# Another order for the beginning of a linear-attention and gated-MLP kernel on one Trainium2 core

## The chip, the cores and the metric

The kernel runs on one core of a Trainium2 chip. The metric is the device time of one execution in microseconds. The core has a matrix engine (TensorE, PE in the profile, with its weight loads as PEld), three elementwise engines (VectorE or DVE, ScalarE or ACT, GpSimd or POOL) and SyncE (SP), which issues nearly all transfers here. Each engine works through its own list of instructions in order and waits on semaphores that others raise.

## The reference

Eight batches of 576 tokens, 8 heads of 64. First a linear attention with a norm per head, then a gated MLP with a spatial gate:

```python
kv = np.einsum('bhsd,bhse->bhde', k, v)
out = np.einsum('bhsd,bhde->bhse', q, kv)
rms = np.sqrt(np.mean(out * out, axis=-1, keepdims=True) + 1e-06)
x = out / rms * g_norm                        # per token: 8 heads side by side, 512 wide
h = gelu_tanh(x @ w_in)                       # 512 -> 1024
u, v = h[..., :512], h[..., 512:]
v_n = layer_norm(v) * g_ln
v_s = np.einsum('ts,bsd->btd', w_sg, v_n) + b_sg[None, :, None]
return x + (u * v_s) @ w_out                  # 512 -> 512
```

The result is float32. `w_in` and `w_out` are float64 inputs: the kernel loads them as pairs of 32-bit words and makes float32 values from them on the chip.

## The kernel before, in words

All large products run as three products of rounded parts: each operand is split into a high part (a cast to the matrix engine's fast float32 form) and a low remainder (a subtraction), and high x high, high x low and low x high are summed in PSUM. Tensors lie with channels on the 128 partitions, so x of a batch is four tiles of 128 channels by 576 tokens, and a token half is 288 columns.

The work of one batch, by the letters of the table `ORDER`: k loads k and v, K multiplies them to kv (four blocks of 128 tokens and a last one of 64), c copies kv out of PSUM; q loads q, o multiplies q by kv, e squares the result, f scales it by g_norm into x, s sums the squares per head with a matrix of ones, t makes 1/rms of the sums, M or r spread it over the channels, x multiplies it in, X and Y make x's high and low parts; U and V are the two halves of x @ w_in, S is the spatial product, G the gate, P the last product, Q and Z add it to x, O stores. D, A, B, E, L, C, F, I load and convert the weights: D is the load, A, B, E, L, C make float32 values from the words (on ACT, DVE and POOL), F the high part, I the low one. N is a warm matmul: it multiplies zeros into a PSUM bank that nobody reads.

`ORDER` (line 115 on) is a table written by hand: the program is recorded in that order, so it sets the order in every engine's list, SP's included. `HOMES` says which buffer each new tile takes; a tile waits until the last user of its buffer is done. A letter at a step's end (v, a, p) names its engine.

In batch 0 the tokens are treated in two halves. o(0, n) makes half n // 4 of channel tile n % 4; `sums` collects the four tiles of a half in one PSUM block (lines 463 to 476), `rstd` (line 494 on) makes 1/rms with one ACT step and three DVE steps, `broadcast` (line 548 on) spreads it over 128 channels with the 0/1 matrix `ext` as the stationary operand. All other batches send 1/rms through DRAM and load it back spread.

The beginning in the table before: k and v of batch 0 are loaded block by block with one block of u's words between them, then all of q; all four tiles of half 0 and those of half 1 follow each other closely; u's first step comes after both halves are scaled and after kv of batch 1 and its first o. The k and v of the last 64 tokens are two loads of 64 partitions each, and `ext` is a load of 64 partitions on SP.

Of the kernel before, what the change touches and what calls it, by code (L numbers as in the profile page):

```python
# [58 lines left out]
""",  # L59
    h="""  # L60
# [775 lines left out]
```

## Time and profile before

| | us |
|---|---|
| median of 3 runs | 494.47 |
| lowest, highest run | 493.2, 494.67 |
| span of the profiled execution, first to last instruction | 490.1 |
| PE busy in it | 482.1 (98%) |
| DVE, ACT, POOL busy | 351.3, 179.8, 159.1 |

The time of the profiled execution outside its span is not in the profile; the median run is 4.37 us above the span. The page also cuts the span into 40 slices: PE shows 6 tenths in the first slice and 9 (90% or more) in all others but the last. The chain of work that ended last is PE for 96% of the span and a transfer of k and v for 2%. A line like "L666" is a line of the kernel; a bracket behind an instruction gives the idle time of its engine before it and what ended that. A PE record of a plain float32 matmul counts twice, as it takes two passes. Times in brackets of another engine's rows are idle time there, which costs nothing unless PE waits for what follows.

### The profile page before, as it was taken

To read this page: it belongs to the slowest core of one execution; us is meant where nothing else is said; L and a number is where in the kernel's file an instruction comes from. 1 tells how busy PE (TensorE), PEld (TensorE's weight loads), DVE (VectorE), ACT (ScalarE), POOL (GpSimd) and SP (SyncE) were. 2 spreads that over 40 slices of the span, in tenths; PEclk is the share of its full clock that TensorE was granted. 3 is DMA by queue.
4 is the path that set the end of the run, shared out by engine and by line. 5 is a ranking of instruction groups with operands and counts; after the bars stand their busy time and mean duration, and the time that the engine had idled before them with its cause. 6 is when DMAs were issued, how large, how long until landed. Compare 5 with 4: busy or idle time off the path is not lost.

```text
span 490.1 us, 10060 instructions
## 1 busy us (share of the span) xinstructions
PE 482.1 (98%) x3989; PEld 440.8 (90%) x3989; DVE 351.3 (72%) x809; ACT 179.8 (37%) x442; POOL 159.1 (32%) x204
## 2 busy tenths in 40 slices
PE   6999999999999999999999999999999999999997
PEld 6668889998998999988998998998998899998997
DVE  1698698888777786468765875577767687577576
ACT  1668575155234331142223323335033332123220
POOL 0333142652232323332143113342305232442551
PEclk9999999999999999999999999999999999999999
DMA  8996793054343612064535443300331021100033
GB/s 228 361 353 232 220 277 104 2 157 141 104 142 89 142 43 74 1 192 130 175 75 185 117 104 117 100 1 1 97 104 49 1 62 43 49 1 0 2 122 120
DMA packets 33658, 55.36 MB, mean 113 GB/s; under 512 B 7308, under 2 KB 9228, under 8 KB 33612
## 3 DMA queue, kind: packets, MB, share of 16 engines
q1 hardware_dynamic: 33612, 54.73, 37.1%
q8 instruction: 31, 0.51, 0.4%
q14 instruction: 15, 0.12, 0.1%
HBM read 44.76 MB, written 9.95 MB: 112 GB/s over the span
## 4 chain that ended last, share of the span: by engine, by line
PE 96%; DMA 2%; DVE 0%; ACT 0%; SPq 0%; issue 0%
PE pu L666 21%; PE pg L680 21%; PE pv L615 20%; PE py L741 18%; PE pkv L414 5%; PE pg L683 3%; PE po L439 3%; PE pss L484 2%; DMA kv_first<-in_vx 1%; DMA kv_first<-in_kx 1%; PE psq L468 1%; PE pq L439 1%; PE pb L552 1%; PE warm L270 0%; SPq L405 0%
## 5 line engine op out<-in xcount | busy, mean ns | idle before, releaser
L693 POOL TENSOR_TENSOR u<-gt,u 128x288 f32<-128x288 f32 x64 | 56.3, 890 | 116.3 <-DVE gt L688 113.6
L680 PE MATMUL pg<-wsh,vh 128*128 128x288 f32 x256 | 75.8, 296 | 0.0
L680 PE MATMUL pg<-wso,vh 128*128 128x288 f32 x256 | 75.4, 294 | 0.0
L680 PE MATMUL pg<-wsh,vo 128*128 128x288 f32 x256 | 75.4, 294 | 0.0
L754 DVE SCALAR_TENSOR_TENSOR x<-py,x 128x288 f32<-128x288 f32 x112 | 49.4, 451 | 28.7 <-PE py L741 28.3
L709 DVE TENSOR_TENSOR g<-u,g 128x288 fp32r<-128x288 f32 x112 | 56.2, 517 | 15.7 <-ACT g L230 13.0
L688 DVE SCALAR_TENSOR_TENSOR gt<-pg,glt,b_bc 128x288 f32<-128x288 f32 x64 | 32.3, 512 | 35.2 <-PE pg L683 34.9
L741 PE MATMUL py<-g,woh 128*128 128x288 f32 x256 | 55.9, 295 | 0.0
L230 ACT CAST g<-u 128x288 fp32r<-128x288 f32 x75 | 30.8, 434 | 68.2 <-POOL u L693 52.3
L671 ACT ACTIVATE u<-pu 128x288 f32<-128x288 f32 x64 | 25.7, 411 | 68.3 <-PE pu L666 67.1
L680 PEld LDWEIGHTS pg<-wsh,vh 128*128 128x128 f32 x256 | 48.2, 188 | 0.8 <-DVE gt L688 0.4
L680 PEld LDWEIGHTS pg<-wso,vh 128*128 128x128 f32 x256 | 48.1, 188 | 0.1
L680 PEld LDWEIGHTS pg<-wsh,vo 128*128 128x128 f32 x256 | 48.1, 188 | 0.0
L666 PE MATMUL pu<-xh,wuh 128*128 128x288 f32 x256 | 45.5, 299 | 0.0
L721 POOL TENSOR_TENSOR u<-u 128x288 f32<-128x288 f32 x33 | 29.4, 894 | 49.6 <-DVE g L709 40.9
L666 PE MATMUL pu<-xo,wuh 128*128 128x288 f32 x256 | 44.3, 295 | 0.0
L666 PE MATMUL pu<-xh,wuo 128*128 128x288 f32 x256 | 44.3, 295 | 0.0
L620 ACT ACTIVATE hv<-pv 128x512 f32<-128x512 f32 x32 | 19.0, 598 | 66.5 <-PE pv L615 59.5
L741 PEld LDWEIGHTS py<-g,woh 128*128 128x128 f32 x256 | 42.7, 188 | 0.6 <-issue 0.4
L741 PE MATMUL py<-g,wxh 128*128 128x288 f32 x192 | 41.5, 295 | 0.0
L666 PEld LDWEIGHTS pu<-xh,wuh 128*128 128x128 f32 x256 | 37.6, 188 | 3.7 <-issue 1.9
L741 PE MATMUL py<-g,woo 128*128 128x288 f32 x128 | 37.8, 295 | 0.0
(123 smaller groups left out, 1005.6 us busy)
## 6 DMA issues: line engine op xcount, KB each, us to landing
q<-in_qT SPq DMA_DIRECT2D x32, 288.0 KB, 5.5
out_y<-x SPq DMA_DIRECT2D x28, 288.0 KB, 2.9
bc<-rd SPq DMA_DIRECT2D x28, 256.0 KB, 3.9
k<-in_kx SPq DMA_DIRECT2D x24, 256.0 KB, 4.9
v<-in_vx SPq DMA_DIRECT2D x24, 256.0 KB, 4.8
kv_first<-in_kx SPq DMA_DIRECT2D x8, 256.0 KB, 6.3
kv_first<-in_vx SPq DMA_DIRECT2D x8, 256.0 KB, 5.4
words<-in_wu SPq DMA_DIRECT2D x4, 512.0 KB, 8.4
```

What stands on the lines that cost most here:

```text
L230: e.copy(dst, src) if e is ac else e.tensor_copy(dst, src)
L414: nc.tensor.matmul(part["kv", b][64 * r : 64 * r + 64, n * 64 : n * 64 + 64], k_[b, c][:, h], v_[b, c][:, h], start=(c == 0 and n == 0), s ...
L615: nc.tensor.matmul(pv, a[cc], w[:, cc, :], start=(n == 0), stop=(n == 11))
L666: nc.tensor.matmul(pu[:, :HS], w[:, cc, f], a[b, cc][:, t], start=(i == 0), stop=(i == 11))
L671: ac.activation(u_[b, n], part["u", b, n][:, :HS], AF.Gelu_apprx_tanh, scale=W_UP)
L680: nc.tensor.matmul(ps[:, :HS], a[:, d], w[:, c, t], start=(i == 0), stop=False)
L688: ve.scalar_tensor_tensor(g_[b, n], ps[:, :HS], glt[:, dc : dc + 1], b_bc[:, half(n // 4)], op0=ALU.mult, op1=ALU.add)
L693: po.tensor_tensor(u_[b, n], g_[b, n], u_[b, n], op=ALU.mult)
L709: ve.tensor_tensor(lo, src, f32(hi), op=ALU.subtract)
L721: e.tensor_tensor(dst, x, y, op=ALU.subtract)
L741: nc.tensor.matmul(y_[b, bank][c][:, :HS], wo_block(h, blk, e)[:, block(c)], a, start=(start and i == 0), stop=(i == 5), skip_group_check= ...
L754: ve.scalar_tensor_tensor(xs, y_[b, bank][c][:, :HS], W_UP, xs, op0=ALU.mult, op1=ALU.add)
```

## The change

The table `ORDER` is written anew for the beginning (to the middle of batch 1's steps), with engines chosen step by step from there on, and `HOMES` with it. The code around it changes in these places:

- u's words of the first 256 columns (D00, D01) are loaded ahead of k and v, the second 256 columns later. Half 0 of batch 0's tokens goes ahead through o, squares, sums, 1/rms, broadcast, scaling and splitting; the first u step (U00, which needs half 0 and the first 128 columns only) stands before half 1 is scaled.
- q of half 1 gets buffers of its own (from the `x` group).
- The sums of a half lie in two column blocks of 144 tokens each, so four blocks for both halves; 1/rms then works on 64 partitions of 144 columns, where it was 32 of 288, and the broadcast takes two matmuls of 144 columns for one of 288. `ext` is 128 partitions, zeroed by POOL, its ones loaded by four small loads that ACT issues.
- The last 64 tokens of k and v come in one load `kvl` of 128 partitions (heads in two groups of partitions, k and v side by side), and the last kv block uses two diagonal tiles of the matrix.
- More steps can choose their engine (A, y, w, G, J, W), and nine of the layer-norm steps y go to ACT.

```diff
-WARM = "po1"
+WARM = "po0"
 ORDER = """
-    k01 k02 k04 D21 F21 D23 D02 A02 E02 B02v L02 C02 F02v I02v k00 N899 ... K00 k03 D00 K01 K02 K03 K04 c00a ...
+    D01 B01v N899 N898 N897 N896 N895 N894 A01v E01 D00 A00a B00a E00 N893 ... k00 K00 ... k02 k01 K01 k03 k04 ...
...
+    ext = T([P, 2, NP * P], F32, "wsh", nm="ext")
     def constants():
+        po.memset(ext, 0.0)
+        for j in range(4):
+            ac.dma_start(ext[32 * j : 32 * j + H, j % 2, :], ex)
...
-        elif n == 22:
-            part["ext"] = T([64, NP * P], F32, "hv_left", nm="ext")
-            sy.dma_start(part["ext"], ex)
...
     def load_kv(b, c):
-        if c < NC and b < 2:
+        if c == NC:
+            k_[b, c] = T([P, 2, C // 2], F32, "k", 3)
+            sy.dma_start(k_[b, c], kvl[b])
+            return
+        if b < 2:
             k_[b, c], v_[b, c] = (t[:, c, :] for t in first[b])
...
+                    else:
+                        k, v = (k_[b, c][64 * r : 64 * r + 64, i, n * 64 : n * 64 + 64] for i in range(2))
...
-                        tile_position=(0, 64 * r),
+                        tile_position=(64 * r if c == NC else 0, 64 * r),
...
-        q_[b, p] = T([P, S], F32, *(("q", 4) if b else ("xh", NP)), nm="q")
+        q_[b, p] = T([P, S], F32, *(("q", 4) if b else ("xh", NP) if p < 2 else ("x", 12)), nm="q")
...
-            nc.tensor.matmul(
-                sums_[0, r][32 * r : 32 * r + 32, :HS],
...
-                tile_position=(0, 32 * r),
-            )
+            for j in range(2):
+                at = 64 * r + 32 * j
+                nc.tensor.matmul(
+                    sums_[0, r][at : at + 32, :QS],
+                    ones[:, ZO - 2 * p : ZO - 2 * p + 32],
+                    part["sq", 0, 2 * p + r][:, j * QS : j * QS + QS],
...
+                    tile_position=(0, at),
+                )
...
     def broadcast(b, n):
-        r = slice(32 * (n % 2), 32 * (n % 2) + 32)
...
+        r = slice(64 * (n % 2), 64 * (n % 2) + 64)
+        for j in range(2):
+            nc.tensor.matmul(
+                pb[:, j * QS : j * QS + QS],
+                ext[r, j, block(n // 2)],
+                part["rstd0"][0][r],
...
-    def v_norm(b, c):
+    def v_norm(b, c, e):
         mv, rs = st_[b, c]
-        ve.tensor_scalar(hv_[b, c], hv_[b, c], mv[:, 0:1], rs[:, 0:1], op0=ALU.subtract, op1=ALU.mult)
+        if e is ac:
+            e.activation(hv_[b, c], hv_[b, c], AF.Identity, scale=rs[:, 0:1], bias=mv[:, 2:3])
+        else:
+            e.tensor_scalar(hv_[b, c], hv_[b, c], mv[:, 0:1], rs[:, 0:1], op0=ALU.subtract, op1=ALU.mult)
```

What this does to the engines' lists shows at three places. The first is SP's list from its fifth transfer on, before. The names are those of the loads' tiles (`k_92` and `v_93` are the 64-partition ends of k and v, `words` are weights as 32-bit words, `gnt` and `glt` small vectors).

```order
L405 DMA k_92<-in_kl 64x512
L405 DMA v_93<-in_vl 64x512
L295 DMA gnt_65<-in_gn 128x1
L300 DMA glt_67<-in_gl 128x4
L287 DMA words_100<-in_wu 128x2x512
L405 DMA kv_first_77<-in_kx 128x512
L405 DMA kv_first_78<-in_vx 128x512
```

And SP's list from its first transfer on, in the change; between the second and the third fence row below stand the other six loads of k and v.

```order
L294 DMA words_94<-in_wu 128x2x512
L294 DMA words_107<-in_wu 128x2x512
L415 DMA kv_first_77<-in_kx 128x512
L415 DMA kv_first_78<-in_vx 128x512
...
L408 DMA k_205<-in_kvl 128x512
L445 DMA q_233<-in_qT 128x576
L302 DMA gnt_65<-in_gn 128x1
L445 DMA q_244<-in_qT 128x576
L294 DMA words_258<-in_wu 128x2x512
L445 DMA q_288<-in_qT 128x576
```

Two blocks of u's words moved ahead of all of k and v, the vector `gnt` of g_norm moved behind the first q, and the two 64-partition loads became one.

The second place is PE's list from the first kv block of batch 0 to the second o of batch 1, before:

```order
L270 MATMUL warm<-zeros 128x256 x46
L414 MATMUL pkv<-kv_first 64x64 x32
L414 MATMUL pkv<-v,k 64x64 x8
L270 MATMUL warm<-zeros 128x256 x11
L439 MATMUL pq<-q,kvf 64x288 x10
...
L552 MATMUL pb<-rstd,ext 128x288 x6
L414 MATMUL pkv<-kv_first 64x64 x32
L414 MATMUL pkv<-v,k 64x64 x8
L439 MATMUL po<-q,kvf 64x288 x8
L666 MATMUL pu<-xh,wuh 128x288 x4
```

And PE's list for the same stretch in the change, from its first warm matmuls to the first o of batch 1, behind which the second u step follows (the first one's 12 matmuls are three rows, of which the first stands here):

```order
L277 MATMUL warm<-zeros 128x256 x58
L428 MATMUL pkv<-kv_first 64x64 x8
L277 MATMUL warm<-zeros 128x256 x7
L428 MATMUL pkv<-kv_first 64x64 x24
L428 MATMUL pkv<-k 64x64 x8
...
L484 MATMUL psq<-sq,ones 32x144 x8
...
L569 MATMUL pb<-rstd,ext 128x144 x8
...
L689 MATMUL pu<-xh,wuh 128x288 x4
...
L569 MATMUL pb<-rstd,ext 128x144 x6
...
L453 MATMUL po<-q,kvf 64x288 x8
```

The first u step moved ahead of the last four broadcasts, of the last two kv blocks of batch 1 and of its first o; warm matmuls moved to the front (58 and 7, then 3 and 1, where it was 46, 11, 3 and 9).

The third place is DVE's list in the change, from the scaling of half 0's last two tiles to the last of its four remainders; `rstd_280` and `rstd_279` are here those of half 1, and the first of them waits for ACT's list, where its step stands behind two word steps of another block.

```order
L582 TENSOR_TENSOR x_286<-x_286,pb_330 128x288
L582 TENSOR_TENSOR x_268<-x_268,pb_339 128x288
L520 TENSOR_TENSOR rstd_280<-rstd_279 64x144
L333 TENSOR_SCALAR w64_348<-w64_348 128x512
L601 TENSOR_TENSOR xo_393<-x_266,xh_326 128x288
L522 SCALAR_TENSOR_TENSOR rstd_280<-psq_343,rstd_280 64x144
L601 TENSOR_TENSOR xo_398<-x_312,xh_328 128x288
L601 TENSOR_TENSOR xo_400<-x_286,xh_396 128x288
L524 SCALAR_TENSOR_TENSOR rstd_279<-rstd_280,rstd_279 64x144
L601 TENSOR_TENSOR xo_403<-x_268,xh_381 128x288
```

Before, the same place of DVE's list, from the first scaled tile on, has half 1's 1/rms steps between the first tile's scaling and its cast, and seven scalings (the first three stand here) ahead of the next remainders:

```order
L565 TENSOR_TENSOR x_283<-x_283,pb_323 128x288
L506 SCALAR_TENSOR_TENSOR rstd_287<-psq_306,rstd_287 32x288
L508 SCALAR_TENSOR_TENSOR rstd_286<-rstd_287,rstd_286 32x288
L230 CAST xh_343<-x_283 128x288
L326 TENSOR_SCALAR w64_346<-w64_346 128x512
L330 SCALAR_TENSOR_TENSOR w64_346<-words_330,w64_346 128x512
L584 TENSOR_TENSOR xo_352<-x_283,xh_343 128x288
L565 TENSOR_TENSOR x_265<-x_265,pb_356 128x288
L565 TENSOR_TENSOR x_279<-x_279,pb_341 128x288
L565 TENSOR_TENSOR x_279<-x_279,pb_362 128x288
```

So half 0 now goes through as a group of four, with half 1's steps woven between its remainders.

## Rows read from the trace of the kernel before

**Rows 1.** The page: the span, and busy time of each engine.

```profile
span 490.1 us, 10060 instructions
...
PE 482.1 (98%) x3989; PEld 440.8 (90%) x3989; DVE 351.3 (72%) x809; ACT 179.8 (37%) x442; POOL 159.1 (32%) x204
```

**Rows 2.** Busy time by stretch: us, each engine's busy (x instructions), granted clock, DMA share, GB/s.

```profile
12.39:34.55 22.16, 21.50 (x263) 13.90 (x263) 17.53 (x40) 13.69 (x33) 6.86 (x6) 1.00 1.04 355
34.55:53.20 18.65, 18.65 (x229) 16.82 (x225) 14.30 (x31) 14.95 (x36) 5.55 (x4) 1.00 0.76 254
```

**Rows 3.** Timeline of TensorE to 39 us: start, length, line, out<-in, xcount, [idle before].

```profile
1.80 8.31 PE L270 MATMUL warm<-zeros 128*128 128x256 f32 x46 [1.80 <-DVE eps L259]
12.39 2.26 PE L414 MATMUL pkv<-kv_first 128*64 128x64 f32 x64 [2.29 <-DMA kv_first<-in_vx]
14.58 0.68 PE L414 MATMUL pkv<-v,k 64*64 64x64 f32 x16
...
16.69 1.69 PE L439 MATMUL pq<-q,kvf 64*64 64x288 f32 x20
...
18.86 2.13 PE L468 MATMUL psq<-sq,ones 128*32 128x288 f32 x8
...
27.42 2.91 PE L552 MATMUL pb<-rstd,ext 32*128 32x288 f32 x12 [0.19 <-DVE rstd L508]
...
33.42 1.20 PE L439 MATMUL po<-q,kvf 64*64 64x288 f32 x16 [0.47 <-ACT kvf L230]
34.56 0.79 PE L666 MATMUL pu<-xh,wuh 128*128 128x288 f32 x4
...
36.34 1.20 PE L439 MATMUL po<-q,kvf 64*64 64x288 f32 x16
37.47 1.41 PE L484 MATMUL pss<-sq,ones 128*32 128x144 f32 x32
```

**Rows 4.** Busy time by stretch again, for the DMA's rate (last column) in the beginning.

```profile
0.00:12.39 12.39, 8.31 (x46) 8.13 (x47) 1.68 (x11) 2.15 (x3) 0.19 (x4) 1.00 0.84 227
...
3.00:7.00 4.00, 4.00 (x21) 4.00 (x20) 0.00 (x0) 0.00 (x0) 0.00 (x0) 1.00 0.95 249
7.00:9.00 2.00, 2.00 (x17) 2.00 (x16) 0.00 (x0) 0.00 (x0) 0.00 (x0) 1.00 1.09 176
13.00:21.00 8.00, 8.00 (x111) 5.46 (x108) 4.25 (x9) 4.13 (x11) 2.59 (x2) 1.00 1.04 389
25.00:27.00 2.00, 2.00 (x13) 1.50 (x12) 1.56 (x5) 1.98 (x5) 0.00 (x0) 1.00 1.07 247
```

**Rows 5.** Timeline of ScalarE: the first four squares.

```profile
17.44 1.32 ACT L451 ACTIVATE sq<-pq 128x288 f32<-128x288 f32 x4 [0.62 <-PE pq L439]
```

**Rows 6.** Groups by line and shape: xcount, busy us, mean ns, idle before.

```profile
L709 DVE TENSOR_TENSOR g<-u,g 128x288 fp32r<-128x288 f32 x112 | 56.2, 517 | 15.7 <-ACT g L230 13.0 <-PE py L741 1.9
...
L754 DVE SCALAR_TENSOR_TENSOR x<-py,x 128x288 f32<-128x288 f32 x112 | 49.4, 451 | 28.7 <-PE py L741 28.3
...
L333 POOL TENSOR_TENSOR w<-w,words 128x512 int32<-128x512 int32 x8 | 11.1, 1387 | 33.3 <-DVE w L330 29.8 <-ACT sq L451 2.0 <-ACT words L320 1.5
...
L330 DVE SCALAR_TENSOR_TENSOR w<-words,w 128x512 int32<-128x512 int32 x8 | 5.5, 688 | 0.2
...
L315 ACT ACTIVATE w<-words 128x512 f32<-128x512 f32 x8 | 5.4, 676 | 9.7 <-DMA words<-in_wu 9.7
...
L326 DVE TENSOR_SCALAR w<-w 128x512 int32<-128x512 int32 x8 | 3.4, 422 | 2.2 <-ACT w L315 2.2
...
L584 DVE TENSOR_TENSOR xo<-x,xh 128x288 fp32r<-128x288 f32 x7 | 3.0, 452 | 0.3 <-ACT xh L230 0.3
...
L459 ACT ACTIVATE x<-pq,g 128x288 f32<-128x288 f32 x5 | 2.5, 494 | 0.0
...
L514 DVE TENSOR_SCALAR rstd<-pss 128x144 f32<-128x144 f32 x7 | 2.2, 308 | 3.7 <-PE pss L484 3.6
...
L502 ACT ACTIVATE rstd<-psq,eps 32x288 f32<-32x288 f32 x2 | 1.0, 484 | 0.5 <-PE psq L468 0.5
```

More of the change, by code (lines that the diff above doesn't have):

```diff
@@ new lines @@
+    f00v q02 o05 f03a e03 q03 o06 o07 o04 e01 e07 f07v f04a f05a N836 N835 N834 M04 x04v M02 x02v X02v X04v M00 x00v
+    C03 F03a I03p e05 M06 x06v s04 D05 A05a B05a s05 s06 s07 t04 t05 E05 k10 K10 k11 K11 X06a k12 K12 Y02v t06 X00a
+    Y04v Y00v t07 Y06v U00 M03 D02 f01a A02a E02 L02 M05 M07 x07v B02a C02 L05 F02v k13 K13 k14 K14 N833 D04 q10
+    A04a E04 M01 x01v I02p c10a B04a X07a Y07v q11 o10 f10a f16v e12 X01a C05 L04 x05v x03v e14 f12a e10 f14a U03
+    e16 q13 q12 o11 e11 s10 e13 s11 e15 s12 e17 s13 t10 t11 U02 m0 t12 t13 X03a Y03v n02 X05a t14 Y05v D06 t15 t16
@@ L398, in load_kv @@
     def load_kv(b, c):
-        if c < NC and b < 2:
+        if c == NC:
[3 more added lines that the diff above has]
+        if b < 2:
             k_[b, c], v_[b, c] = (t[:, c, :] for t in first[b])
         else:
-            n = P if c < NC else LT
-            k_[b, c], v_[b, c] = T([P, C], F32, "k", 3)[:n], T([P, C], F32, "v", 3)[:n]
-        for t, whole, last in ((k_[b, c], kx, kl), (v_[b, c], vx, vl)):
-            sy.dma_start(t, whole[b, :, c, :] if c < NC else last[b])
+            k_[b, c], v_[b, c] = T([P, C], F32, "k", 3), T([P, C], F32, "v", 3)
+        for t, whole in ((k_[b, c], kx), (v_[b, c], vx)):
+            sy.dma_start(t, whole[b, :, c, :])
     def kv(b, n):
@@ L495, in rstd @@
         if b == 0:
-            r, n = slice(32 * (n // 4), 32 * (n // 4) + 32), n % 4
+            r, n = slice(64 * (n // 4), 64 * (n // 4) + 64), n % 4
             if "rstd0" not in part:
-                part["rstd0"] = [T([64, HS], F32, t, nm="rstd") for t in ("xlh", "xlo")]
+                part["rstd0"] = [T([P, QS], F32, t, nm="rstd") for t in ("xlh", "xlo")]
             y, a = (t[r] for t in part["rstd0"])
-            sums = sums_[0, r.start // 32][r, :HS]
+            sums = sums_[0, r.start // 64][r, :QS]
             if n == 0:
@@ L510, in rstd @@
         if n == 0:
-            part["rstd"] = [T([P, QS], F32, t, nm="rstd") for t in ("hv_left", "ry", "bl")]
-        m, y, a = part["rstd"]
+            part["rstd", b] = [T([P, QS], F32, t, nm="rstd") for t in ("hv_left", "ry", "bl")]
+        m, y, a = part["rstd", b]
         if n == 0:
@@ L550, in broadcast @@
         pb = part["pb", n] = PS("pb")
-        r = slice(32 * (n % 2), 32 * (n % 2) + 32)
-        nc.tensor.matmul(
-            pb[:, :HS],
-            part["ext"][r, block(n // 2)],
-            part["rstd0"][0][r],
-            start=True,
-            stop=True,
-            skip_group_check=True,
-            tile_position=(r.start, 0),
-        )
+        r = slice(64 * (n % 2), 64 * (n % 2) + 64)
[4 more added lines that the diff above has]
+                part["rstd0"][0][r],
+                start=True,
+                stop=True,
+                skip_group_check=True,
+                tile_position=(r.start, 0),
+            )
     def scale(b, n, e):
@@ L610, in v @@
         else:
-            xs = [part["xlh"][:, p, :] for p in range(NP)], [part["xlo"][:, p, :] for p in range(NP)]
+            xs = [part["xlh", b // 2][:, p, :] for p in range(NP)], [part["xlo", b // 2][:, p, :] for p in range(NP)]
         n = 0
@@ L682, in s @@
         for w in (w4[1 - r], w4[r]):
-            nc.tensor.matmul(ps[:, :HS], part["vl", r][:, d], w[:, t], start=False, stop=w is w4[r])
+            nc.tensor.matmul(ps[:, :HS], part["vl", b // 2, r][:, d], w[:, t], start=False, stop=w is w4[r])
     def gate_bias(b, n):
@@ L811 @@
     vx, vl = tokens(v)
[L812 to L815 removed]
+    kvl = np.stack([kl.reshape(B, LT, 2, 2, P), vl.reshape(B, LT, 2, 2, P)], 2)
+    kvl = con(kvl.transpose(0, 4, 1, 2, 3, 5).reshape(B, P, 2, C // 2))
+    ex = np.zeros((H, NP * P), np.float32)
+    for h in range(H):
+        ex[h, h * 64 : h * 64 + 64] = 1.0
     qT = q.reshape(B, NP, 2, 2, HS, D).transpose(0, 3, 1, 5, 2, 4)
```

246 lines of the change are left out of this document (122 added, 124 removed), and 31 rows, old and new, of tables (h, ps).

## The prediction

> **What bounds the kernel now.** I read the page first: TensorE (PE) is busy for 482.1 of the span's 490.1 us [rows 1]. Then the busy time by stretch [rows 2]: from 34.55 us on PE has no idle time, before it PE is idle or kept busy with dummy work. The end therefore moves only by what PE loses before 34.55 us, or by a stall that the change makes later. Third, PE's timeline of the beginning [rows 3]. Nothing useful runs before 12.39. Then come kv of batch 0, the q products (pq), the sums of squares (psq), their broadcast (pb), kv of batch 1, the first half of batch 1's q products (po, 33.42), the first u step (pu, 34.56); the second po starts at 36.34. By 36.34 PE has done exactly the list that the change does before its second u step (PE's rows in the section on the change), so 36.34 is the mark: how much earlier the change reaches it is what it gains, if nothing stalls after it. Between 12.39 and 34.55 stand 23 warm matmuls and waits on a chain of small steps: a 288-column psq block takes 2.05 us, then ACT's rstd step and three DVE steps before pb can run.
>
> The median of the runs, 494.47, lies 4.37 us above the profiled span of 490.1. What lies around the span is taken as unchanged, so a gain in the span is taken off 494.47.
>
> **The new chain, step by step.** All times from the span's start.
> (1) First kv. The change puts 58 warm matmuls ahead instead of 46. The 46 end at 10.11; later ones come every 0.118 us (17 in 2.00 us, [rows 4]), so 12 more end at 11.5. kv's 80 records took 2.8 us (12.39 to 15.19, of it 2.26 plus 0.61), and 7 warm matmuls in the middle take 0.95 with their shape change: kv ends at 15.25, against 15.19. Is the data there? 1.05 MB of u's words now stand ahead of k and v, so the last load is in place when 3.41 MB have moved (two loads of 512 KB, nine of 256). Before, 2.81 MB had moved by 12.39 (227 GB/s), including a dip to 176 GB/s at 7 to 9 us, where the 64-row loads of k's and v's ends stand in the queue; 389 is the rate without them [rows 4]. The same dip, 247, comes at 25 to 27, where batch 1's ends stand. With one 128-row load I put 389 in its place: 0.43 MB more, so 3.41 MB at 12.8. The load that ended PE's old wait was there at 12.39 [rows 3] with 2.36 MB up to and including itself (six loads of 256 KB, two of 128, one of 512), while 2.81 had moved: landing comes 0.45/0.389 = 1.15 us after its place in the stream. So 13.95, before kv's last block needs it (14.6). If the single load dips too, 15.0, and the chain slips 0.4.
> (2) q products. After kv the copy takes 0.47 (PE's wait at 33.42): pq starts at 15.75, against 16.69. q's first half (4.0 MB moved at 14.3, landed 15.45) is just there.
> (3) Squares. The first began 0.75 after pq, four took 1.32 [rows 3, 5]: done at 17.85. The sums go into four column blocks, two at a time. Not shown before for two blocks; with four blocks (pss) 16 matmuls take 1.34 us, 0.34 a group. Bounds: 0.34 a pair, or 0.51, what one 288-column matmul took; I take 0.34 as pss is the nearest row. Only the last pair stands on the path, so it counts 0.34 instead of the old 2.05 of a whole block.
> (4) A wait that the change adds: ACT's scaling of x (f02, f06) needs g, which DVE makes only behind word block 3. That block lands when 4.52 MB are through: 12.8 + 1.11/0.389 + 1.15 = 16.8; DVE then needs 0.42 + 0.42 + 0.69 and two single-column steps, some 0.3: 18.6 [rows 6]. ACT's two scalings, 0.49 each, end at 19.6, and behind them stands rstd. On 144 columns it is not shown: between 0.31 (DVE's 144-column step) and 0.48 (ACT's 288-column step); I take 0.35. So 19.95; three DVE steps at 0.31: 21.0. pb's first bank is free after two more ACT steps and a word step (0.68 + 0.49 + 0.33): 21.45. pb starts at 21.5, against 24.74.
> (5) First u step. It needs four scaled, rounded pieces of x and their four remainders (xo). On DVE, ahead of the remainders, now stands a step of the second half's rstd (t05), which waits for ACT's t04, and that stands behind e01, e07, f04, f05, a cast, e05 and two word steps: 0.66 + 0.99 + 0.68 + 0.33 + 1.36 = 4.0 us after 21.45, plus 0.35: 25.85. Then DVE: 0.31 + 0.42 + 4 x 0.45 + 2 x 0.31 = 3.15: 29.0 [rows 6]. PE meanwhile does pb, the other sums and three kv blocks of batch 1, and can start u by 27: the last remainder ends it, at 29.15.
> (6) To the mark. Three pb (0.49 each, 1.45), two kv blocks (1.1), a warm one and the last pb (0.65), po (1.13): 33.5. The copy of kv lies beside the last pb; batch 1's q (9.63 MB: 12.8 + 6.22/0.389 + 1.15 = 29.95) has landed.
> The mark moves from 36.34 to 33.5: **2.85 us gained**, 494.47 - 2.85 = 491.6.
>
> **What else the change edits.** pb goes from 8 matmuls of 288 columns to 16 of 144: the same columns, taken at nothing; at worst 0.34 for each of 16 against 0.49 for 8, 1.5 us. kv's last block on two diagonal tiles: 0.61 before, between 0.55 (the rate of a 128-row block) and 0.7 now, taken at nothing. One load fewer per batch costs and gains nothing once PE is full. Nine normalisations move from DVE to ACT (not shown on ACT), three of the four remainders of u's weights to POOL, seven gates from POOL to DVE: none is on PE's path as long as PE always finds its next matmul ready, as it does from 34.55 us on, and a late one costs PE up to its own length, 0.45 on DVE to 1.39 on POOL. POOL's memset and ACT's four small loads of ext lie ahead of any word. Behind ACT's cast of block 0, which waits for POOL, stands the kv copy: POOL's two adds and a remainder (3 x 1.39) from about 8.6 end by 13, 2 us before it is needed.
>
> **Rivals.** *Handed back.* DVE is late again behind the mark: it must give the second half's remainders, the last parts of v's weights and batch 1's scaled x, each wanted 3 us sooner. In these steps DVE shares the beginning with more POOL work. For it: a 128x288 step with both inputs in SBUF takes 517 ns (L709), the same shape with one from PSUM 451 (L754), and POOL's word steps are 1.39 long [rows 6]. Against: DVE sheds nine normalisations and three weight remainders. Price: the four remainders of step 5 at 0.07 to 0.9 more each, 0.3 to 3.6; at 2.4 the time is 494.0, within what can be told.
> The Trainium skill, "SBUF — State Buffer", section "Who interferes with whom", has the rule that speaks against this edit: a DVE instruction with two SBUF inputs contends with a GpSimd instruction that reads SBUF, the pair being a lock held for a whole instruction. By that rule each remainder could wait out one POOL step; the mean of 66 ns in the rows says that this is rare.
> *Slower: the clock.* Of PE's 6.2 us from 15.3 to 21.5 only 3.9 hold work (two pq groups at 1.13, psq 1.34, three warm matmuls), and 11 warm matmuls are left behind the first kv against 23. If the granted clock falls to its lower level there, kv of batch 1, u, pb and po cost twice: from 3 to 7 us a warm matmul came every 0.19 (21 in 4.00 us), from 7 to 9 every 0.118 [rows 4]. From the first u step to the end of the second one that is 1.6 + 1.45 + 1.1 + 0.65 + 1.13 + 1.6 = 7.5 us more: 499. It decides from 4.4 us of lost PE time on. The column of the granted clock is 1.00 in both stretches, so that it need not show such a fall; the pace of the matmuls does. Against: behind the 2.29 us wait before 12.39 kv came at 0.565 a block (2.26 / 4), no slower than the 0.61 of its smaller last block [rows 3].
> The Trainium skill, "TensorE: Matmul & The Clock Gate", section "Why this matters for your kernels", warns of idle gaps between bursts of matmuls, after which the clock is halved; no row of this case shows where that begins.
> *More than forecast.* If t04 comes sooner than reckoned, PE itself ends u at 27.8: 1.3 more, 490.3. *Not what it says*: half the tokens are no use if the first u step waits for the whole chain anyway. Then it starts after all eight pb as before, and 1.8 us of pb and the second rstd come back: 493.4.
>
> **How the numbers follow.** Forecast, 489.2 to 493.0, including more than forecast: 0.60. Handed back, or not what it says, 492.4 to 495.9: 0.29, of it 0.06 below 493.0. Slower by the clock, up to 499, or by a longer stall: 0.11. What a measurement here can tell from no change is 0.3%, 1.5 us: faster means below 493.0. So faster 0.66, same 0.23, slower 0.11. The range 489.2 to 495.0 leaves out the slower case, the end of the handed back one and the best tail.
>
> **What would show it.** In the profile of the changed kernel: first kv at 11.5 and its end at 15.25; pb at 21.5; the first pu started before 28 and its last matmuls held by DVE's xo until 29; the second pu at 33.5; no PE idle time behind it; no dip of the DMA rate at a k load. Wrong if PE waits behind 34 us, if the DMA is late at kv, or if the granted clock drops.

## The result: slower, and the profile after

The change is slower: a median of 501.29 us (500.34 to 503.47, 4 runs) against 494.39 for the kernel before on the same chip, a ratio of 1.0146 [1.0106, 1.0187]. The forecast was 491.6, in a range of 489.2 to 495.0. The profiled execution of the change took 501.09, its span 499.3; 1.8 us lie outside the span, and 1.7 to 2.0 in every later timed run.

The page of the change, span and engines:

```profile
span 499.3 us, 10133 instructions
...
PE 486.1 (97%) x4021; PEld 443.5 (89%) x4021; DVE 349.9 (70%) x803; ACT 181.6 (36%) x439; POOL 171.4 (34%) x223
```

Against [rows 1] the span is 9.2 us longer, and PE is idle for 13.2 us instead of 8.0. The timeline of TensorE in the change answers to [rows 3] (start, length, line, out<-in, xcount, [idle before]):

```profile
1.80 8.86 PE L277 MATMUL warm<-zeros 128*128 128x256 f32 x58 [1.80 <-DVE eps L266]
10.58 0.69 PE L428 MATMUL pkv<-kv_first 128*64 128x64 f32 x16
...
13.11 1.15 PE L428 MATMUL pkv<-kv_first 128*64 128x64 f32 x32 [0.82 <-DMA kv_first<-in_vx]
15.74 1.10 PE L428 MATMUL pkv<-kv_first 128*64 128x64 f32 x16 [1.48 <-DMA kv_first<-in_vx]
16.77 1.12 PE L428 MATMUL pkv<-k 64*64 64x64 f32 x16
18.36 2.20 PE L453 MATMUL pq<-q,kvf 64*64 64x288 f32 x16 [0.47 <-ACT kvf L233]
20.49 2.13 PE L484 MATMUL psq<-sq,ones 128*32 128x144 f32 x16
...
25.27 2.19 PE L569 MATMUL pb<-rstd,ext 64*128 64x144 f32 x16 [0.17 <-DVE rstd L524]
...
30.05 0.79 PE L689 MATMUL pu<-xh,wuh 128*128 128x288 f32 x4
...
36.51 1.20 PE L453 MATMUL po<-q,kvf 64*64 64x288 f32 x16
37.64 0.79 PE L689 MATMUL pu<-xh,wuh 128*128 128x288 f32 x4
```

PE waits twice for k and v, 0.82 and 1.48. The first 16 records of q products then take 2.20 where 20 took 1.69 before. The windows of the change show the clock there (columns as in [rows 2]; the granted clock is the third from the end):

```profile
13.11:15.80 2.69, 1.21 (x34) 1.11 (x36) 0.19 (x1) 0.62 (x1) 1.82 (x2) 1.00 1.00 317
15.80:22.62 6.82, 6.35 (x68) 3.83 (x70) 2.18 (x6) 2.58 (x7) 0.00 (x0) 0.50 1.03 367
```

From 15.80 to 22.62 the clock is at its lower level of 1.2 GHz, behind a stretch in which PE was busy for 1.21 of 2.69 us. The second u step, the mark, comes at 37.64: 1.30 later than before, 4.14 later than forecast.

The larger part of the loss lies behind the mark. From the mark to the end, first the kernel before:

```profile
36.34:60.00 23.66, 23.66 (x243) 20.80 (x243) 18.39 (x41) 17.65 (x42) 5.78 (x5) 1.00 0.74 229
...
sum 453.76, PE 450.51 PEld 417.16 DVE 330.39 ACT 162.15 POOL 151.14; mean PE 112.63 PEld 104.29 DVE 82.60 ACT 40.54 POOL 37.78
```

and the change:

```profile
37.64:61.30 23.66, 21.86 (x210) 19.08 (x207) 17.05 (x44) 18.37 (x46) 8.00 (x6) 1.00 0.63 173
...
sum 461.66, PE 453.50 PEld 417.56 DVE 331.12 ACT 165.62 POOL 160.80; mean PE 113.38 PEld 104.39 DVE 82.78 ACT 41.41 POOL 40.20
```

453.8 us before, 461.7 after: 7.9 more, and 1.30 + 7.9 are the 9.2. Before, PE's only idle time there is the 3.25 us of the end. In the change the waits of PE are (waited for: us in total, times, longest):

```profile
PE pkv L428 <- DMA kv_first<-in_vx: 2.3, 2, 1.5
...
PE py L764 <- DVE x L777: 1.5, 1, 1.5
PE pv L632 <- ACT wvh L233: 1.0, 1, 1.0
PE pu L689 <- ACT u L694: 0.8, 1, 0.8
PE pu L689 <- ACT hv L637: 0.7, 1, 0.7
...
PE pg L706 <- DVE vl L681: 0.4, 1, 0.4
```

All but the first lie behind the mark, between 46 and 152 us. Counted from the start of each matmul to the start of the next, against the median of the same pair of shapes in both traces, the change loses 7.9 us behind the mark: 1.52 (py), 1.08 (pv), 0.95 and 0.90 (pu), 0.91 (pg), 0.70 (a pv at 151) and 0.29 (at 285) are 6.4 of it, at seven places; the rest are many small delays.

### The profile page after: what moved, and what is told of

It reads as the page before. It is cut to its first block, busy times and chain, and to the rows that moved or that the text cites. A ratio compares the mean times of both kernels' runs of the same rounds, so it can differ in the third digit from the quotient of the medians.

```text
span 499.3 us, 10133 instructions
## 1 busy us (share of the span) xinstructions
PE 486.1 (97%) x4021; PEld 443.5 (89%) x4021; DVE 349.9 (70%) x803; ACT 181.6 (36%) x439; POOL 171.4 (34%) x223
## 4 chain that ended last, share of the span: by engine, by line
PE 79%; DVE 8%; DMA 5%; ACT 4%; issue 2%; POOL 1%; SPq 0%; DVEq 0%; POOLq 0%; ACTq 0%
PE pg L703 19%; PE pu L689 17%; PE py L764 17%; PE pv L632 15%; PE pg L706 3%; PE pkv L428 3%; PE po L453 3%; DMA kv_first<-in_vx 3%; DMA bc<-rd 2%; PE pss L500 1%; DVE x L585 1%; DVE xo L601 1%; DVE g L732 1%; DVE woo L393 1%; PE pq L453 1%
## 5 line engine op out<-in xcount | busy, mean ns | idle before, releaser
L716 POOL TENSOR_TENSOR u<-gt,u 128x288 f32<-128x288 f32 x57 | 49.9, 885 | 107.4 <-DVE gt L711 104.7
L233 ACT CAST g<-u 128x288 fp32r<-128x288 f32 x72 | 29.7, 434 | 76.9 <-POOL u L716 43.1
L744 POOL TENSOR_TENSOR u<-u 128x288 f32<-128x288 f32 x34 | 30.9, 911 | 45.4 <-DVE g L732 36.6
L764 PE MATMUL py<-g,wxh 128*128 128x288 f32 x192 | 41.8, 296 | 1.5 <-DVE x L777 1.5
L689 PEld LDWEIGHTS pu<-xo,wuh 128*128 128x128 f32 x256 | 37.7, 188 | 0.7 <-DVE xo L601 0.7
```

Source lines behind the costliest of these rows:

```text
L233: e.copy(dst, src) if e is ac else e.tensor_copy(dst, src)
L689: nc.tensor.matmul(pu[:, :HS], w[:, cc, f], a[b, cc][:, t], start=(i == 0), stop=(i == 11))
L716: e.tensor_tensor(u_[b, n], g_[b, n], u_[b, n], op=ALU.mult)
L744: e.tensor_tensor(dst, x, y, op=ALU.subtract)
L764: nc.tensor.matmul(y_[b, bank][c][:, :HS], wo_block(h, blk, e)[:, block(c)], a, start=(start and i == 0), stop=(i == 5), skip_group_check= ...
```

## The experiments

All kernels were timed in five rounds beside the kernel before (medians 493.5 to 494.4). The tables of the order name a step by a letter, batch or block and place: `N` is a warm matmul, `K` a kv block, `k` and `q` loads, `A B C E F L` the steps on a block of words, `D` its load. Two theories for 1.30 + 7.9: *the beginning* (late k and v, the clock behind it, DVE beside POOL), from which the rest follows; or *two separate losses*, the beginning's and one in the new order of ACT's and DVE's lists further on.

**Warm matmuls in the two kv waits.** 17 more keep PE busy there.

```
-k02 k01 K01 k03 k04 K02 K03
+k02 k01 N600 ... N605 K01 k03 k04 K02 N620 ... N630 K03
```

> The changed kernel with 17 more warm matmuls in the two places where PE waits for blocks of k and v: 6 ahead of the second block, 11 ahead of the fourth (0.82 and 1.48 us of waiting in the trace of the change; a warm matmul takes 0.118). Theory A, the clock: the waits made the granted clock fall to half at 15.8 us, and that costs 3.9 us on the chain (kv's last two blocks 1.10 + 1.12 where 0.56 + 0.61 is the full rate, psq 2.13 where 1.17 is). With PE kept busy the granted clock stays 1.00, the first pb starts at 21.5 to 22.5 (25.27 in the change), the second u step at 33.8 to 34.8 (37.64), and the time falls by about 3, to 497.5 to 499. Theory B, handed back: the beginning gets shorter in the same way, but ACT and DVE are the ones who are late behind it, so that PE's waits after 40 us grow by what was won; the time stays within 1 us of 501.3. Theory C: the chain is held by ACT's wait for g and by the loads, the clock only hides that; then pb starts at 24 or later at a clock of 1.00 too.

499.85, 1.0128 [1.0094, 1.0162]. The clock stays at 1.00, the 16 psq fall from 2.13 to 0.74 + 0.68, and the mark comes at 36.41, 1.23 earlier. So the clock's fall is real and is worth 1.2 us of this loss, not the 3 that theory A put on it: the first pb starts at 24.02 at a clock of 1.00, as theory C has it. From the mark to the end it is 461.7 again, with the same waits in the same places:

```profile
36.41:498.10 461.69, 453.37 (x3672) 417.66 (x3668) 332.89 (x757) 165.74 (x405) 160.68 (x211) 1.00 0.31 95
```

The 7.9 does not follow from the beginning.

**Loads of k and v first**, u's words behind them, and, in a second kernel, q as well and g earlier.

```
-D01 B01v N899 ... D00 A00a B00a E00 ... k00 K00 ... k02 k01 K01 k03 k04
+k00 k02 k01 k03 k04 D01 D00 B01v N899 ... A00v B00v E00 L00 ...
```

> The changed kernel with all loads of k and v ahead of the two blocks of u's words, as far as the first five token groups go; word block 0's scaling steps and its cast go to DVE so that ACT's copy of kv does not wait behind them. Theory A: the words ahead of k and v made the data late (2.36 MB are needed before the last kv block where it was 3.41). kv then runs without PE's waits of 0.82 and 1.48 and ends by 13.5 (17.8 in the change), the clock stays 1.00, the second u step starts by 34, the time is 496.5 to 499. Rival: the dip in the DMA's rate (160 to 230 GB/s between 9 and 12 us in the change, at no 64-row load) belongs to k's and v's own loads; then it comes earlier, kv still waits for its fourth block, and the clock falls as before: 500 to 502.

> The changed kernel with k, v and the first two q loads ahead of u's words, g and word block 3 as in the kernel with g early, word block 0's scaling on DVE and its cast on ACT behind half 0's 1/rms, and warm matmuls in PE's short waits. The loads of k and v alone ahead of the words ended kv at 15.4 instead of 17.8, but q came at 18.2 and g at 26.8 behind the words. Theory A (the words ahead of k, v and q are what made the beginning late): kv ends by 15.5, pq starts by 16.2, the first pb at 20 to 21.5, the first u step waits for word block 0 or starts by 26.5, the second one starts by 34; the time is 1.5 to 4 below the filled kernel's 499.85. Rival: the chain through the words is as long as the one through kv, and the first u step starts at 28.8 as in the filled kernel, whatever comes first: 499 to 501.

509.89 (1.0313) and 504.46 (1.0216). kv ends at 15.4 and 15.9, but the words come late, DVE works on them when g is wanted, and PE waits 4.35 and 1.76 us for ACT's scaled x (mark 46.5 and 41.8). Ahead of that it waits 2.77 and 1.17 for q. What is won at k and v is lost at q and g. Both miss.

**POOL's steps of word block 3 put later**, out of the way of DVE's 1/rms steps. In the change these two rows, DVE's and POOL's timelines, collide:

```profile
23.49 0.30 DVE L522 SCALAR_TENSOR_TENSOR rstd<-psq,rstd 64x144 f32<-64x144 f32 x1
23.82 1.30 DVE L524 SCALAR_TENSOR_TENSOR rstd<-rstd 64x144 f32<-64x144 f32 x1
```

```profile
23.68 1.29 POOL L340 TENSOR_TENSOR w<-w,words 128x512 int32<-128x512 int32 x1 [8.74 <-DMA kv_first<-in_kx]
```

The DVE step with one input from PSUM takes 0.30, the one with both in SBUF, started 0.14 behind POOL's, 1.30: it ends 0.15 behind POOL. The Trainium skill, "SBUF — State Buffer", section "Who interferes with whom", states this (two SBUF inputs against a GpSimd instruction that reads SBUF, the first to issue holds the port), and the trace agrees.

```
-x00v C03 F03a I03p e05
+x00v e05 ... t07 C03 F03a I03p Y06v
```

> The changed kernel with word block 3's add, cast and remainder (two of them on POOL, at 23.7 and 26.7 us in the change) recorded behind half 0's splitting, so that POOL is idle while DVE makes 1/rms and the casts. Theory A, contention: DVE's 64x144 step took 1.30 beside POOL's add (0.30 alone) and two casts 1.33 beside POOL's remainder (0.62 alone); without POOL there they take 0.30 and 0.62, the first pb starts 1.0 earlier (24.3), the first u step ends 1.0 to 1.7 earlier (31 to 31.7), and the time is 499.6 to 500.4. Rival: these are late by something else and the second u step, which needs word block 3 too, waits for its remainder: within 0.5 of 501.3, or slower.

502.24, 1.0169 [1.0143, 1.0195]. POOL's add, with nothing ahead of it in its list, still ran beside the 1/rms step (the add from 24.54, the step from 24.70 for 1.30); its remainder now met two xo (1.83 for both, 0.45 each alone), and PE waited 1.05 for xo, where it had waited 0.15. The lock moved; it did not go.

**The nine normalisations y back to DVE**, the rest as in the change.

> The changed kernel with the nine normalisation steps that it gives to ACT back on DVE. In the change PE waits behind the second u step for ACT (0.79 at 47.7, 1.01 at 55.3, 0.74 at 111.3, 0.17 at 151.7) and for DVE (0.45 at 84.9, 1.5 near 123). Theory A: the steps are too much for ACT there; the wait at 111.3 goes and the time falls by 0.7 to 1.5 (499.8 to 500.6). Rival: both are late from the beginning on, the first two waits lie ahead of any of these steps and stay as they are, and DVE, now 5 us longer, makes the wait near 123 longer by 0.5 or more: 501.3 to 503.

506.0, 1.0250 [1.0221, 1.0279], above the rival's 503 too, and 465.1 from the mark on: DVE is fuller, and PE waits 2.2 for ACT's u, which stands behind a cast that waits 4.5 for DVE's hv. This edit of the change was worth some 3.4 us (465.1 - 461.7); it is not the cause.

**ACT's table of gelu loaded early** (token `i`), on top of the warm matmuls. ACT in the change, in front of the first gelu:

```profile
45.30 0.67 ACT L233 CAST w4a<-wl 64x576 fp32r<-64x576 f32 x1
45.98 1.28 ACT L694 ACT_TABLE_LOAD   x1
47.28 0.41 ACT L694 ACTIVATE u<-pu 128x288 f32<-128x288 f32 x1
```

```
-I02p c10a
+I02p i c10a
```

> The kernel with the filled waits (17 more warm matmuls, 499.85) and one edit more: ACT loads its table for gelu ahead of the copy of batch 1's kv, where it sits idle for 2.90 us (31.5 to 34.4), and not at the first gelu at about 45 us, where the 1.28 us load ends one of PE's waits (0.80). Theory A, a list too long for ACT behind the second u step: the wait of 0.80 goes, and with 1.28 less in ACT's list the cast that ends the wait of 1.03 at 54 comes sooner too; the waits at 110 and 123 stay. The time falls by 0.8 to 1.8, to 498.1 to 499.1. Rival: these waits are set by DVE and POOL, and ACT only passes them on; then the second one stays at 1.0 and the time falls by 0.8 at most.

498.88, 1.0108 [1.0081, 1.0136]. The wait for u is gone, 460.3 from the mark on: one of the seven places, 1.4 us, shown (0.95 of it at the place itself). The next wait, for wvh, only shrinks from 1.03 to 0.87.

**DVE instead of POOL for the two steps that hold up DVE before the 1.5 wait.** In the change `g<-u,g` at 121.86 takes 1.52 beside POOL's `vo<-hv,vh` (121.59, 1.48); alone it takes 0.45. The two rows, and the first of them again with the remainder on DVE (the kernel below):

```profile
121.86 1.52 DVE L732 TENSOR_TENSOR g<-u,g 128x288 fp32r<-128x288 f32 x1
121.59 1.48 POOL L676 TENSOR_TENSOR vo<-hv,vh 128x512 fp32r<-128x512 f32 x1
```

```profile
120.17 0.44 DVE L734 TENSOR_TENSOR g<-u,g 128x288 fp32r<-128x288 f32 x1
```

```
-w12p ... R01p
+w12v ... R01v
```

> The kernel with the filled waits and two POOL steps that the change or the order put beside DVE's work given to DVE: the remainder of v of batch 1's third block (POOL 1.48 at about 121, beside it a DVE step of 0.45 took 1.52) and one combining step (POOL 0.88 at about 108.5, beside it a DVE remainder of 0.69 took 1.30). DVE then has 0.69 + 0.44 more to do itself. Theory A, contention: DVE's steps there come back to 0.45 and 0.69 and the waits of PE for DVE of 1.45 near 123 and of 0.74 near 110 shrink by at least half each; the time falls by 1 to 2, to 497.9 to 498.9. Rival: DVE simply has too much to do there; then its list is as long as before, the waits stay within 0.3 and the time within 0.5 of 499.85.

501.49, 1.0159 [1.0134, 1.0184]. The 1.45 wait falls to 0.38 and the 0.74 for hv to 0.13, as expected; but DVE now has the steps itself:

```profile
PE pg L705 <- DVE vo L678: 1.9, 1, 1.9
...
PE pkv L430 <- DMA v<-in_vx: 0.6, 1, 0.6
```

and behind that wait, at 128.37, the clock falls:

```profile
126.50:128.37 1.87, 0.02 (x1) 0.00 (x0) 1.80 (x6) 0.00 (x0) 0.00 (x0) 1.00 0.38 123
128.37:131.80 3.43, 3.43 (x15) 3.43 (x16) 1.72 (x5) 0.00 (x0) 0.00 (x0) 0.53 0.34 98
```

So DVE's steps beside POOL's made the 1.5 wait; moving the work between the two handed it back, with 463.7 from the mark on.

**g earlier**: word block 3's steps on DVE behind g and 1/rms.

```
-D03 A03v E03 L03 F21a f02a ... t02 B03a t03 ... e03 q03
+D03 F21a f02a ... t02 t03 A03v E03 L03 ... e03 B03a q03
```

> The kernel with the filled waits, with g made as soon as its load is there and word block 3's steps on DVE and ACT behind half 0's 1/rms (its add on POOL follows them). In the kernel with the filled waits alone ACT waits 0.50 for g (until 20.60) and a DVE step of 1/rms takes 1.29 beside POOL's add (0.30 alone); first pb at 24.0. Theory A: both are on the chain; 1/rms starts on ACT right behind psq (20.9), the first pb comes at 22.3 to 22.8, the second u step at 34.7 to 35.5 (36.4), and the time falls by 0.9 to 1.7. Rival: word block 3 is now late for the second u step, which then waits for its remainder: no change or slower.

499.64, 1.0117 [1.0100, 1.0134], mark 36.05: the first pb came 1.1 earlier, but PE then waited for DVE's scaled x; alone it gains 0.4 at the mark.

**Six casts of g and weights from DVE to ACT**, on top of the table load.

```
-H00v h04v h03v F34v F35v h02v
+H00a h04a h03a F34a F35a h02a
```

> The kernel with the filled waits and the early table load (498.88), with six casts of 0.3 us that stand in DVE's list between 95 and 123 us given to ACT, which is idle for 3.9 and 2.4 us there. In the chain of waits of that kernel DVE is the chain without a break from 95.3 to 108.2 and from 117.4 to 121.4. Theory A, DVE's list is too long there (its work, and 3.8 us by which its steps are longer beside POOL's): with 1.8 us less to do the waits of PE at 109 (0.75) and 121 (1.45) shrink by 1.0 to 1.8 together and the time falls by as much, to 497.1 to 497.9. Rival: what DVE wins is lost again in the next wait, as when two POOL steps were given to DVE (a wait of 1.85 came at 128); the time stays within 0.5.

497.15, 1.0063 [1.0041, 1.0084]. The 1.5 wait for DVE is gone, DVE now waits 2.56 for PE at that place: with less work of its own DVE is in time although POOL's step is still there, so both had their part in that wait; 0.6 for ACT's sq is new. By the ratios 2.2 us won, by the spans behind the mark 0.5 (460.3 to 459.8); between these the size stays open.

**Parts of the change put into the kernel before.** 18 warm matmuls ahead of its first kv; the sums in four blocks alone, with ext zeroed by POOL and loaded by four loads of ACT; and the sums with ext loaded by SP in its old place.

```
+po.memset(ext, 0.0)
+for j in range(4):
+    ac.dma_start(ext[32 * j : 32 * j + H, j % 2, :], ex)     # second kernel; third: sy., at D22
```

> The kernel before with 18 more warm matmuls ahead of its first kv block, where PE waits 2.29 us for the data in the trace. Its timed runs show a mean granted clock of 0.995 to 0.997 and spans of 491.3 to 493.9, where the profiled one had 0.999 and 490.1. Theory A: in most runs the clock falls behind that wait, for some 3.4 us, which costs 1 to 2 us; with PE kept busy the granted clock is 0.998 or more in every run, the first pq starts at 16.7 as in the trace, and the median falls by 1 to 2 us (ratio 0.996 to 0.998). Rival: the clock falls somewhere else, or the spread comes from the loads; no change within 0.3%, or slower by up to 0.5 where the warm matmuls outlast the wait.

> The kernel before with one part of the change alone: sums of batch 0 in four blocks of 144 columns, 1/rms on 64 partitions, broadcast by two matmuls of 144, ext zeroed by POOL and its ones loaded by ACT. Two blocks of 288 columns took 2.13 each in the trace of before, two pairs of 144 took 1.17 each in the trace of the change. Theory A: both stand on PE's path, so the last pb starts 0.6 to 1.5 earlier (27.42 before), the mark (second po, 36.34) at 34.9 to 35.8, and the time is 0.6 to 1.5 below before. Rival: ACT's scaling stands ahead of 1/rms (20.28 to 21.46) and the casts behind pb are DVE's (x ends at 31.7), so that PE waits elsewhere: within 0.3%; slower if ACT's small loads or POOL's zeroing delay the first words.

> The kernel before with the sums in four blocks, and ext's ones loaded by four small loads that SP issues where it loaded ext before. With ACT's loads at the start the same kernel made no difference (ratio 1.0005): its first kv started 1.9 later than before, but from kv's end to the second po it took 19.9 where before took 21.15. Theory A: without the hold-up the first kv starts at 12.4 as before and the 1.27 are left: 0.8 to 1.5 below before (ratio 0.997 to 0.9985). Rival: the sums gain nothing by themselves, ratio 0.999 to 1.001.

493.26 (0.9975 [0.9954, 0.9996]), 494.27 (1.0005 [0.9986, 1.0024]), 492.63 (0.9973 [0.9957, 0.9990]). PE in the second kernel:

```profile
14.29 3.92 PE L417 MATMUL pkv<-kv_first 128*64 128x64 f32 x64 [5.34 <-DMA kv_first<-in_vx]
...
38.83 1.20 PE L442 MATMUL po<-q,kvf 64*64 64x288 f32 x16
```

With ACT's four loads in front, the first kv comes at 14.29 instead of 12.39 [rows 3], and takes 3.92 instead of 2.26: the granted clock is 0.50 from 11.79 to 18.62. The rest of the chain, from the end of kv to the mark, is shorter: 19.8 against 21.1. SP's list shows how: it stands still from 3.89 to 6.81 (first fence), where the longest stand in the kernel before is 0.93 (second).

```profile
3.41 0.48 SPq L408 DMA_DIRECT2D v<-in_vl  x1
6.81 0.33 SPq L301 DMA_DIRECT2D gnt<-in_gn  x1
```

```profile
5.40 0.47 SPq L405 DMA_DIRECT2D kv_first<-in_kx  x1
6.80 0.33 SPq L405 DMA_DIRECT2D kv_first<-in_vx  x1
```

With the loads given to SP the first kv is at 10.96. With the 18 warm matmuls, which keep the clock at 1.00, kv ends at 17.93 with ACT's loads and at 14.89 with SP's. From the mark to the end it is 453.7 to 453.8 in each of them, as before. With ACT's loads and the 18 warm matmuls together it was 494.03 (0.9999); ext by SP and the warm matmuls gave no more than either:

> The same with the wait ahead of the first kv block filled by 18 warm matmuls. Theory A: the two gains add (0.9975 and 0.998): ratio 0.993 to 0.997, the fastest so far. Rival: they overlap, 0.9965 to 0.999.

492.50, 0.9972 [0.9952, 0.9993]. So three small versions are faster than the kernel before, by 0.25 to 0.28%: the intervals end below 1, and the size is just under the 0.3% that was taken as the limit.

Their profiles do not show this gain: the marks are 36.70, 36.48 and 36.67, that of the kernel before is 36.34. In the kernel with ext on SP, kv ends at 14.56, but PE then waits 0.71 for DVE's scaled x and 1.12 for batch 1's k and v, so that 21.9 lie between kv's end and the mark, and the 1.27 that its theory counted on are not there. The timed runs tell more. Of 110 runs of the kernel before, 14 have a mean clock of 0.999 or 1.000 and a mean span of 491.0, and 83 a clock of 0.995 to 0.997 and 492.2. With the 18 warm matmuls 9 of 12 runs are at the higher value, with 491.0 too. So the warm matmuls win back the clock, though not in every run. The sums with ext on SP have spans of 490.2 and 490.9 at these two values (four and six runs): some 0.8 and 1.2 are theirs, and where isn't shown.

**ext by SP in the change.**

```
-        for j in range(4):
-            ac.dma_start(ext[32 * j : 32 * j + H, j % 2, :], ex)
+        elif n == 22:
+            for j in range(4):
+                sy.dma_start(ext[32 * j : 32 * j + H, j % 2, :], ex)
```

> The changed kernel with one edit: the four small loads of ext's ones, which ACT issues at the start, are issued by SP behind the last q load of batch 0. In the changed kernel SP stands still from 3.19 to 4.53 and from 4.86 to 7.23 ahead of its next loads of k and v; in the kernel before with the sums in four blocks (and so with ACT's small loads) SP stood still from 3.89 to 6.81, the DMA's rate fell to 37 GB/s behind that, and the first kv started at 14.29 (12.39 before). Theory A: the four small loads hold up SP's loads; without them SP issues its first ten or so loads by 6, kv ends by 16 (17.82), the clock falls less or not at all, the second u step starts at 34.5 to 36 (37.64), the time is 498.5 to 500 (501.29). Rival: SP waits for its own first loads to land, whatever ACT does; kv ends within 0.5 of 17.8, the time stays within 1 of 501.3.

PE's timeline:

```profile
13.45 1.15 PE L430 MATMUL pkv<-kv_first 128*64 128x64 f32 x32 [0.21 <-DMA kv_first<-in_vx]
...
16.53 1.20 PE L455 MATMUL pq<-q,kvf 64*64 64x288 f32 x16 [0.47 <-DMA ext<-in_ex]
```

502.88, 1.0174 [1.0143, 1.0204]: the data came as expected, the time did not. The waits for k and v fall from 2.30 to 0.36 and pq starts 1.8 earlier; but ACT waits 1.4 for g, PE has four waits between 18 and 23.5, and from 24.79 to 28.20 the granted clock is 0.50. The mark is at 37.39. That execution took 501.33; the others have mean clocks of 0.985 to 0.993, where it has 0.996.

**The pieces together**: table load, casts, ext on SP, g early, the 17 warm matmuls taken out again and 4 put behind the first sums; then the same with the kv copy ahead of the v words (A04, E04) in ACT's list. A kernel with the first three and the 17 warm matmuls still in gave 497.36 (1.0062): there the warm matmuls themselves held kv until 17.5.

> The kernel with ext's small loads on SP, the early table load and the casts on ACT (497.36), without the 17 warm matmuls ahead of kv's later blocks (k and v are there in time without ACT's loads, so that these now keep kv back: its end was 17.5), with g made as soon as its load is there and word block 3's steps behind half 0's 1/rms, and 4 warm matmuls behind half 0's sums. Theory A, the chain as predicted, once its loads and g are in time: kv ends by 15.5, pq starts by 16, the first pb at 20.3 to 21.7 (23.6 there), the second u step at 33.3 to 34.8 (35.9), clock 1.00 throughout; the time falls by 1.0 to 2.5, to 494.9 to 496.4. Rival: word blocks, q or the clock take it back; the second u step within 0.5 of 35.9 and the time within 0.7 of 497.4.

> The kernel with the chain in time (495.78), with one step moved: the scaling of word block 4 (v's weights), for whose load ACT stood 3.36 us, is recorded behind ACT's copy of batch 1's kv. Theory A: that was the only thing between the predicted mark and the measured one: PE's wait of 1.64 at 34.3 goes, the clock does not fall there, the second u step starts at 33.3 to 34.3 (36.43 in the profiled run of that kernel), and the time is 494.0 to 495.2. Rival: handed back; v's weights are then later for the first v product, where PE already waits 0.87 at 53, or the waits of 0.64 near 109 and 122 grow, and the time stays within 0.6 of 495.8.

495.78 (1.0028 [1.0008, 1.0047]), where ACT stood 3.36 us for v's words ahead of the kv copy and PE lost 1.64 and the clock; and 494.62 (1.0016 [1.0005, 1.0028]). PE in the last:

```profile
14.78 0.68 PE L430 MATMUL pkv<-k 64*64 64x64 f32 x16
15.93 1.20 PE L455 MATMUL pq<-q,kvf 64*64 64x288 f32 x16 [0.47 <-ACT kvf L234]
...
21.14 0.76 PE L571 MATMUL pb<-rstd,ext 64*128 64x144 f32 x4
...
34.29 0.81 PE L691 MATMUL pu<-xh,wuh 128*128 128x288 f32 x4
```

kv ends at 15.46 (forecast 15.25), pb starts at 21.14 (21.5), the mark is at 34.29 (33.5): the beginning within 0.8 us of the prediction, with the clock at 1.00. And the kernel is still no faster than before, since from the mark to the end it takes 459.0, not 453.8:

```profile
PE pv L634 <- ACT wvh L234: 0.9, 1, 0.9
PE pu L691 <- ACT hv L639: 0.7, 1, 0.7
PE pss L502 <- ACT sq L467: 0.6, 1, 0.6
...
PE pg L708 <- DVE vl L683: 0.5, 1, 0.5
```

| From the mark to the end | us |
|---|---|
| before, and the kernels made of it | 453.7 to 453.8 |
| the change; with warm matmuls; g early; ext on SP; POOL's steps later; loads first | 461.7; 461.7; 461.7; 462.1; 462.1; 461.9 and 461.6 |
| y on DVE; POOL's two steps on DVE | 465.1; 463.7 |
| table load; and casts; and ext on SP; and the whole beginning | 460.3; 459.8; 459.2; 459.0 |

The theory of two separate losses holds: in the kernels that change the beginning alone the mark lies anywhere from 36.05 to 46.5, and 461.6 to 462.1 follow it.

What makes the largest place left, ACT's wvh, was not tested, but the trace of the change names it:

```profile
50.95 3.68 POOL L340 TENSOR_TENSOR w<-w,words 128x512 int32<-128x512 int32 x2 [9.75 <-ACT u L694]
```

```profile
53.42 0.62 ACT L233 CAST wvh<-w 128x512 fp32r<-128x512 f32 x1 [2.54 <-POOL w L340]
54.67 0.62 ACT L233 CAST wvh<-w 128x512 fp32r<-128x512 f32 x1 [0.63 <-POOL w L340]
```

ACT is not behind with its own work there: it stands idle for POOL's two adds of v's words, which follow two word steps of DVE. In the kernel before these adds start at 43.95 and 47.18, and ACT never waits for them. Two parts of the change were not tested by themselves: the new buffers of `HOMES` and the seven gates moved to DVE.

## Why the prediction was wrong

All three signs that the prediction gave for its being wrong came: PE waits behind 34 us, the DMA is late at kv, the clock drops.

**The step that failed most: "none is on PE's path as long as PE always finds its next matmul ready, as it does from 34.55 us on".** That was a row of the kernel before [rows 2], true of its order and taken over to an order that the change rewrote as far as batch 1. In the new order PE lacks an operand at seven places between 46 and 285 us, for 6.4 of the 7.9 us. The *handed back* rival named DVE and the place, but put it on the remainders ahead of the first u (0.3 to 3.6); there the price was 0.2. Shown: one place is ACT's table load, which now stands in PE's way (1.4); one is DVE, short of time and held up by POOL (the 1.5 wait goes with the casts, and with POOL's two steps on DVE, where it comes back at another place). ACT's hv is late for the same reason: that wait, too, goes with POOL's two steps. For ACT's wvh (1.1), DVE's vl (0.9) and ACT's sq (0.7, new with the casts) no kernel moved just those steps. For wvh the trace points at POOL's adds; for the others, and for the small delays among the 5.2 that are left in the last kernel, the cause stays open.

**(1) "POOL's memset and ACT's four small loads of ext lie ahead of any word"**, costed at nothing. They do, and they hold up SP's loads. Where it is shown both ways: ext on ACT moves the first kv of the kernel before by +1.9, and taking it off brings kv's end in the change from 17.89 to 16.06. So of the 2.64 by which kv is late against 15.25, 1.8 are from this: 1.0 for data that come later, 0.85 for kv's last two blocks at the lower clock. The 389 GB/s put for the stretch without 64-row loads was not seen either: the change moved 196 from 9 to 12 us, with k, v and q in 128-row loads alone. So the dips were not those of the 64-row loads; what makes them is open.

**The clock rival came**, with less than it was priced at: 1.2, not 7.5, and below the 4.4 from which by its text it decides the outcome. The clock fell behind 2.3 us of waits for k and v that the prediction did not have, on kv, pq and psq and not on batch 1's kv, u, pb and po; and its column, which the text did not trust, shows it (0.50). From the start of pq to the start of pb it is 6.91 against a forecast of 5.75; with warm matmuls in the waits 5.93.

**(2) and (3) held.** The copy takes 0.47, and the psq pairs of the change behind the clock's return come in 1.17 for four pairs, 0.29 each (0.34 taken). **(4) held in kind:** DVE's g is late, at 20.75 to 20.96 (forecast 18.6), and it is the next bound as soon as kv comes earlier. **(5) and (6) held:** from the start of pb to the mark 12.37 against 12.0, with u's last matmul held by xo, 0.15. The error at the mark is then 2.64 - 0.03 + 1.16 + 0.37 = 4.14.

**The base.** The 4.37 us above the span was taken for what lies around it. It is 1.8; by the other 2.5 the profiled execution was shorter than the median of its runs: these lie between 491.5 and 497.0, mostly at a mean clock of 0.995 to 0.997, where the profile shows 0.999. So by spans the miss is 499.3 - 487.25 = 12.05 (4.14 + 7.9), by medians 9.7, the difference being this.

## What to carry to other kernels

That an engine never waits is a fact of one order of the other engines' lists; where a change rewrites these, ask at each place what the engine waits for next, and price a stretch of "no idle" by the slack that its feeders have, not at zero. Cut the span at a mark that both kernels pass with the same work done, and time both sides: here it told two losses apart at once, and which edits could not touch the larger. A small load on another queue is not free because it is small: look whether the main queue stands still behind it.

## What the runs showed of the hardware

- In the kernel before with ACT's four loads of 16 KB (their issue takes ACT from 1.70 to 5.00) the DMA moved 105 GB/s from 7 to 10 us, against 234 without them. In the change, with the same four loads, it moved 290 there and 196 from 9 to 12. Why the transfers slow down isn't shown.
- The clock fell to its lower level behind two waits of 0.82 and 1.48 us with 1.15 us of matmuls between them, and, with POOL's two steps on DVE, behind one of 1.85. In the profiled execution of the kernel before it did not fall behind one of 2.29, so the length of a wait alone does not tell.
- A cast of 128x288 with one input, too, was held up beside POOL: two took 1.33 at 27.01, and 0.53 where POOL ran elsewhere.
- Two 144-column matmuls in different column blocks run beside each other: 16 records of psq in two column blocks took 1.17, where 8 of 288 columns in one took 2.13, and 32 records of pss in four took 1.41 [rows 3].
